# Banded plus pooled attention feeding a ReGLU feed-forward on one core: slot order moved into tables, one more head pair turned by TensorE

## The chip, the cores and the metric

The kernel runs on one core of a Trainium2 chip. The metric is device time in microseconds from the start to the end of one execution. A time is the median of several executions; the profile is that of one execution of its own. The engines go by these names: PE is TensorE (PEld its weight load), DVE is VectorE, ACT is ScalarE, POOL is GpSimd, SP is SyncE, which here only issues DMAs. "Lnnn" is a line of the kernel. Each engine takes its instructions strictly in the order in which the program lists them, so an instruction that waits holds up everything behind it on its engine.

## The reference

```python
def _attn_ref(q, k, v):                    # (8, 8, 576, 64) each: batch, heads, positions, depth
    factor = 4
    q_d = q.reshape(B, H, Sd, factor, D).mean(axis=3)     # likewise k_d, v_d; Sd = 144
    out_d = sm_attn(q_d, k_d, v_d)                        # softmax attention on the means
    out_up = np.repeat(out_d, factor, axis=2)
    mask = np.abs(pos[:, None] - pos[None, :]) < factor
    scores = np.where(mask, scale * q @ k^T, -1e9)
    out_local = softmax(scores) @ v
    return out_up + out_local

def _moe_ref(x, w_gate, w_val, w_out):     # x: (4608, 512), the heads side by side
    gate = np.maximum(x @ w_gate, 0.0)     # w_gate, w_val: (512, 1536)
    val = x @ w_val
    return gate * val @ w_out              # w_out: (1536, 512)
```

There are two attentions for every head: a local one over a band seven keys wide, and one over means of four positions whose result is repeated four times. Their sum, 4608 tokens by 512, goes through a gated feed-forward net.

## The kernel before

**Pairs.** The 64 heads are worked on as 32 pairs; pair p holds two heads of batch p // 4, and four pairs make a batch. The attention output goes transposed into one SBUF tensor, xT (512 depths by 4608 tokens), from which the feed-forward net reads.

**Two kinds of pairs.** Q and K come from memory with positions on the partitions and have to be transposed, and so do the softmax weights. For pairs p < NPE = 12 TensorE does both (turn_qk_pe, L281: twelve transposes of 96 columns and their copies out of PSUM; turn_en_pe, L521: six transposes of the local weights; turn_ad_pe, L530: five of the pooled weights). For the other pairs a DMA transposes (turn_qk, L272, and turn_a, L513, both issued by SP). TensorE pairs also add the band mask on PE (one matmul a head, L343), which for the others is an addition on DVE (mask_l, L398), and they get the means of V from PE matmuls (pool_v, L373) where the others load V a second time in another layout (load_v4, L223) and add on POOL (sum_v4, L231). For the first NPP = 5 pairs the means of q and k are also made by PE (twelve more small matmuls in turn_qk_pe); from pair 5 on POOL makes them (pool_qk, L325: two additions, L331 and L334).

**Stages of a pair.** load, load_v (SP); cast_qk for q (on ACT, L257, or on POOL, L259, for pairs 2 to 4) and for k (POOL, L259); cast_v (POOL, L270); the turn of q and k; pool_qk; scores (36 small matmuls, L348); scores_d (four, L365); pool_v (L381, L390); shift_l (DVE: maximum and subtraction); copy_vd (ACT); max_d (DVE); exp_l (ACT); exp_d in two halves (ACT); sums and weights_l (DVE); weights_d (a reciprocal on DVE and two multiplications on POOL, L491); the turns of the weights, each with its copy on ACT (L528, L535); outputs (36 small matmuls, L544, then eight or twelve of the pooled part, L567, and a copy on ACT, L575); add_x (DVE, into xT).

**Slots.** One Python function, slot(n), lists the instructions for n from -2 to 33, and the tile framework is told to keep that order on every engine. Slot n works on the scores and softmax of pair n, on casts and turns of pairs n + 1 to n + 3, on loads of pairs up to n + 5, and on the outputs of pair n - 1 (TensorE pairs) or n - 2 (DMA pairs). SP's queue in a slot holds the DMA transposes first, then the loads of one pair (four pieces of q and k for a TensorE pair, then the V windows), then V and the second V of a DMA pair, then the stores of finished rows.

**The feed-forward net.** The 4608 tokens are nine chunks of 512 columns. An h block (ffn_h, L595) is eight matmuls of 512 columns into two PSUM banks for one of the twelve blocks of 128 hidden units of one chunk, a relu on ACT (L608) and a product on DVE (L610). A y block (ffn_y, L614) is twelve matmuls of 512 columns for 128 finished tokens, a copy on ACT (L632) and a store. A list, ffn, gives their order: three h blocks of a chunk, then one y block of the chunk before. ffn_do (L654) takes the next one, or does nothing if the chunk's tokens are not all there: chunk c needs the batch in which its last token lies (`made`, counted in pairs). A slot calls it up to `quota` times (L688: 0 before slot 4, 3 up to slot 13, then 4 or 5), at fixed places; a None in the list uses up a call. What is left after slot 33 runs by itself.

**Weights.** POOL issues the DMAs of the feed-forward weights, which also change the type: a quarter of w_gate and w_val in each of slots 1 to 4 (load_h_weights, L152), a quarter of w_out in each of slots 5 to 8 (load_y_weights, L160), both at the end of POOL's work for the slot.

**Warm-up.** In slots -1 to 3, fill (L681) puts matmuls on a tile of ones between the stages: twelve in slot -1, five in each of slots 0 to 3. They compute nothing that is used.

Of the kernel before, what the change touches and what calls it, by code (L numbers as in the profile page):

```python
# [17 lines left out]
NEG = -1.0e30  # L18
VR = 112


def _np_constants():
# [18 lines left out]
    both = np.concatenate([mask.reshape(96, 228), np.eye(96, dtype=np.float32)], axis=1)  # L41
    both = (both.view(np.uint32) >> 16).astype(np.uint16).view(np.float32)
    return both, pool, np.eye(96, dtype=np.float16)
# [7 lines left out]
def kernel(  # L51
# [23 lines left out]
    NPE = 12  # L75
    NPP = 5

    mask_np, pool_np, eye_np = _np_constants()
    eye_dr = nc.inline_tensor(eye_np, name="eye96").ap()
    mask_dr = nc.inline_tensor(mask_np, name="band_mask").ap()  # L80
    pool_dr = nc.inline_tensor(pool_np, name="pool4").ap()
# [30 lines left out]
    both_sb = cons.tile([96, 162], FP32, name="both_sb")  # L112
    mask_sb = both_sb.bitcast(BF16)[:, 0:228].rearrange("p (b c) -> p b c", b=6)
    eyeb_sb = both_sb.bitcast(BF16)[:, 228:324]
    pool_sb = cons.tile([VR, 256], FP16, name="pool_sb")
    eye_sb = cons.tile([96, 96], FP16, name="eye_sb")
    warm = cons.tile([128, 2], FP32, name="warm")
    nc.vector.memset(warm, 0.0)
    nc.scalar.dma_start(eye_sb, eye_dr)
    nc.scalar.activation(out=warm, in_=warm, func=AF.Exp)  # L120
    nc.scalar.dma_start(both_sb, mask_dr)
    nc.scalar.dma_start(pool_sb, pool_dr)
# [13 lines left out]
    for t in v_t:  # L136
        nc.gpsimd.memset(t[32:64], 0.0)
    ones = xT[:, 3, 0:TCH]
    nc.vector.memset(ones, 1.0)
    nc.vector.memset(v_t[0][0:32, 0, :], 0.0)  # L140
    for t in qk_t:
        nc.gpsimd.memset(t[:, 2 * S :], 0.0)
    for t in wt_t:
        nc.vector.memset(t, 0.0)
    for t in v4_t:
        nc.vector.memset(t[32:64], 0.0)
# [95 lines left out]
    def cast_qk(p, i):  # L242
# [13 lines left out]
        if i == 0 and not 2 <= p < NPP:  # L256
            nc.scalar.copy(out=dst, in_=src)  # L257
        else:
            nc.gpsimd.tensor_copy(out=dst, in_=src)  # L259
# [21 lines left out]
    def turn_qk_pe(p):  # L281
# [7 lines left out]
        for b in range(3):  # L289
# [5 lines left out]
            if b == 1:  # L295
# [5 lines left out]
                nc.vector.tensor_copy(out=o, in_=tp.rearrange("p f (a g) -> p a g f", a=2))  # L301
# [34 lines left out]
    def scores(p):  # L336
# [3 lines left out]

        if p < NPE:
            for t in sp:
                nc.tensor.matmul(out=t, lhsT=eyeb_sb, rhs=mask_sb, start=True, stop=False)  # L343
# [29 lines left out]
    def pool_v(p):  # L373
        if p >= NPE:
# [56 lines left out]
    def copy_vd(p):  # L431
        s = st[p]
        s["vd"] = p_vd.tile([128, 4, D], FP16, name="vd", tag="vd")
        if p < NPE:
# [349 lines left out]
```

## Time and profile before

| | before |
|---|---|
| median of 3 executions | 394.9 us (394.38 to 395.0) |
| the profiled execution's own time | 394.73 us |
| its span, first to last instruction | 393.0 us |
| mean granted TensorE clock | 0.983 |
| PE busy | 372.9 us, 95%, 4612 matmuls |
| DVE busy | 249.7 us, 64%, 618 instructions |
| ACT busy | 206.1 us, 52%, 580 |
| POOL busy | 198.1 us, 50%, 248 |
| DMA | 65.77 MB in 172204 packets, mean 167 GB/s |

The page cuts the span into 40 equal slices; a digit is the busy share of a slice in tenths, for PEclk the clock that was granted to TensorE, for DMA the mean of the core's 16 engines. The chain is followed back from the last instruction: at each step to what released it, or to the instruction before it on its engine; "issue" is time in which the engine waited for nothing that the profile shows. A row of the timeline is start, length, engine, line, operation, output<-inputs, tile shape, count; a bracket behind it is the idle time before the first of them and what ended it. In the list of waits the three numbers are the total in us, the count and the longest. Matmuls are pipelined, so the start of one to the start of the next tells more than the length of one.

### The profile page before, as it was taken

Reading aid. Unit: us, or ns where it says so; the run is one execution under the profiler, and the core shown is the slowest. Engines: PE = TensorE matmul, PEld = TensorE weight load, DVE = VectorE, ACT = ScalarE, POOL = GpSimd, SP = SyncE. Lnnn points to the kernel's source line nnn. Section 1 sums busy time; section 2 is a strip of 40 time slices with the busy share of each in tenths; the row PEclk is TensorE's granted clock in tenths of the full one; section 3 lists DMA queues with packets and bytes.
Section 4 is the critical chain, followed back from the end, with each engine's and each line's share of the span. In section 5 each row is a group of like instructions: output and inputs, shape, how many; then the busy total and the mean of one; then the engine's idle time right before and its main releaser. Section 6 shows DMA issues by size and latency. Waiting matters only on the chain.

```text
span 393.0 us, 11686 instructions
## 1 busy us (share of the span) xinstructions
PE 372.9 (95%) x4612; PEld 190.7 (49%) x4612; DVE 249.7 (64%) x618; ACT 206.1 (52%) x580; POOL 198.1 (50%) x248
## 2 busy tenths in 40 slices
PE   6997889899999999999999999999999999999996
PEld 3675356555554444444444444444444444444443
DVE  4799469888678868775767777777776322232210
ACT  3687468878664555655555555555445323332321
POOL 5598297865689775757475667757631000000000
PEclk9799699999999999999999999999999999999999
DMA  7999999998999999999999999997322000100102
GB/s 187 244 214 218 224 203 248 220 220 185 201 216 227 228 220 243 228 213 217 221 225 218 215 232 229 209 224 143 98 71 73 28 28 30 50 28 27 48 34 107
DMA packets 172204, 65.77 MB, mean 167 GB/s; under 512 B 152742, under 2 KB 165750, under 8 KB 172150
## 3 DMA queue, kind: packets, MB, share of 16 engines
q1 hardware_dynamic: 165974, 60.18, 72.3%
q0 software_dynamic: 5824, 4.72, 7.9%
q8 instruction: 36, 0.59, 0.7%
q10 hardware_dynamic: 352, 0.14, 0.2%
q14 instruction: 18, 0.15, 0.1%
HBM read 48.50 MB, written 9.44 MB: 147 GB/s over the span
## 4 chain that ended last, share of the span: by engine, by line
PE 71%; DMA 13%; DVE 4%; ACT 4%; POOL 3%; issue 2%; SPq 2%; POOLq 0%; ACTq 0%; DVEq 0%
PE h_ps L600 41%; PE y_ps L622 23%; DMA vst<-in_v_dram 9%; DMA nat<-in_k_dram 3%; PE s_ps L348 2%; SPq L182 2%; PE u_ps L544 2%; PE o_ps L567 1%; PE d_ps L365 1%; DVE sm L424 1%; ACT r L608 1%; POOL h L259 1%; DVE mx L423 1%; DVE g L610 1%; DVE s_ps L401 1%
## 5 line engine op out<-in xcount | busy, mean ns | idle before, releaser
L610 DVE TENSOR_TENSOR g<-r,h_ps 128x512 f16<-128x512 f16 x108 | 73.9, 684 | 102.2 <-PE h_ps L600 69.2
L600 PE MATMUL h_ps<-xT,wg_sb 128*128 128x512 f16 x432 | 112.9, 384 | 0.5 <-DVE sm L424 0.5
L600 PE MATMUL h_ps<-xT,wv_sb 128*128 128x512 f16 x432 | 111.8, 382 | 0.6
L622 PE MATMUL y_ps<-wo_sb,g 128*128 128x512 f16 (+1 forms) x444 | 98.5, 374 | 0.2 <-DVE sm L424 0.2
L608 ACT ACTIVATE r<-h_ps 128x512 f16<-128x512 f32 x108 | 64.2, 595 | 39.0 <-PE h_ps L600 38.8
L600 PEld LDWEIGHTS <-wv_sb 128*128 128x128 f16 x432 | 42.3, 98 | 54.4 <-issue 5.3
L622 PEld LDWEIGHTS <-g 128*128 128x128 f16 x444 | 43.0, 98 | 49.6 <-DVE sm L424 0.3
L600 PEld LDWEIGHTS <-wg_sb 128*128 128x128 f16 x432 | 38.5, 98 | 44.0 <-issue 1.7
L499 POOL TENSOR_TENSOR wts<-ed,rd 80x288 f16<-80x288 f16 x40 | 25.8, 663 | 65.4 <-ACT h L257 31.4
L632 ACT COPY y_sb<-y_ps 128x512 f32<-128x512 f32 (+1 forms) x36 | 20.8, 578 | 57.9 <-PE y_ps L622 57.7
L460 ACT ACTIVATE e<-sm 96x456 f16<-96x456 f32 x32 | 18.6, 583 | 58.2 <-DVE sm L424 55.0
L448 ACT ACTIVATE ed<-d_ps,nb 80x144 f16<-80x144 f32 x128 | 47.4, 381 | 0.0
L270 POOL CAST v<-vst 112x1152 f16<-112x1152 f32 x32 | 36.8, 1151 | 12.2 <-DMA vst<-in_v_dram 12.2
L331 POOL TENSOR_TENSOR t<-qkT 128x576 f32<-128x576 f16 x27 | 30.9, 1144 | 6.3 <-DVE qkT L301 5.3
L259 POOL CAST h<-nat 96x768 f16<-96x768 f32 x35 | 29.3, 836 | 5.6 <-DMA nat<-in_k_dram 2.8
L407 DVE TENSOR_REDUCE d_ps<-d_ps 80x2 f32<-80x288 f32 x64 | 28.9, 452 | 1.5 <-PE d_ps L365 1.5
L584 DVE TENSOR_TENSOR xT<-u_ps,od 128x288 f16<-128x288 f32 x64 | 26.0, 445 | 2.9 <-ACT od L575 2.9
L257 ACT CAST h<-nat 96x768 f16<-96x768 f32 x29 | 24.3, 841 | 5.4 <-DMA nat<-in_k_dram 5.4
L423 DVE TENSOR_REDUCE mx<-s_ps 96x6 f32<-96x228 f32 x64 | 24.3, 379 | 3.8 <-PE s_ps L348 3.8
L424 DVE TENSOR_TENSOR sm<-s_ps,mx 96x228 f32<-96x228 f32 x64 | 25.1, 391 | 2.2
L448 ACT ACTIVATION_READ_ACCUMULATOR ed<-d_ps,nb 80x1 f32 x128 | 26.2, 205 | 0.0
L472 DVE TENSOR_TENSOR wts<-e,rl 96x456 f16<-96x456 f16 x32 | 25.1, 786 | 1.1
(59 smaller groups left out, 369.4 us busy)
## 6 DMA issues: line engine op xcount, KB each, us to landing
vst<-in_v_dram SPq DMA_DIRECT2D x62, 216.0 KB, 4.8
out_dram<-y_sb SPq DMA_DIRECT2D x35, 256.0 KB, 3.8
nat<-in_q_dram SPq DMA_DIRECT2D x20, 288.0 KB, 3.7
nat<-in_k_dram SPq DMA_DIRECT2D x20, 288.0 KB, 4.5
v<-in_v_dram SPq DMA_DIRECT2D x40, 144.0 KB, 4.2
nat<-in_q_dram SPq DMA_DIRECT2D x12, 192.0 KB, 5.9
nat<-in_k_dram SPq DMA_DIRECT2D x12, 192.0 KB, 4.8
wg_sb<-in_moe_w_gate_dram POOLq DMA_DIRECT2D x4, 384.0 KB, 8.8
```

The source lines that it names most:

```text
L259: nc.gpsimd.tensor_copy(out=dst, in_=src)
L270: nc.gpsimd.tensor_copy(out=s["v16"], in_=s.pop("vst"))
L331: nc.gpsimd.tensor_tensor(out=t1, in0=qkv[:, :, :, 0], in1=qkv[:, :, :, 1], op=ALU.add)
L407: nc.vector.tensor_reduce(out=nbr, in_=s["dp"][h], axis=AX.X, op=ALU.max)
L423: nc.vector.tensor_reduce(out=mx[:, half], in_=sp, axis=AX.X, op=ALU.max)
L424: nc.vector.tensor_tensor(out=sm[:, half, :], in0=sp, in1=mx[:, half, None].to_broadcast([96, 6, 38]), op=ALU.subtract,)
L448: nc.scalar.activation(out=s["ed"][:, i, :], in_=s["dp"][h][:, c, :], func=AF.Exp, scale=SCALE / 16.0, bias=s["nb"][:, i : i + 1], accum_o ...
L584: nc.vector.tensor_tensor(out=x5[:, :, par], in0=up[par].rearrange("p l (t f) -> p l t f", f=4), in1=od4[:, :, par, :, None].to_broadcast( ...
L600: nc.tensor.matmul(out=h, lhsT=w[:, kk, bass.ts(jj, 128)], rhs=xT[:, kk, bass.ts(c, TCH)], start=(kk == 0), stop=(kk == 3),)
L608: nc.scalar.activation(out=r, in_=h1, func=AF.Relu)
L610: nc.vector.tensor_tensor(out=g, in0=r, in1=h2, op=ALU.mult)
L622: nc.tensor.matmul(out=y, lhsT=gts[c][jj][:, bass.ts(ty, 128)], rhs=wo_sb[:, jj, cols], start=(jj == 0), stop=(jj == NJJ - 1),)
```

## The change

**The order is data.** slot(n) no longer calls the stages one by one. Three tables of words, FIRST for n < 4, MIDDLE for 4 <= n < NPE and LAST for the rest, list the stages; a word names a stage, an offset to n and, behind a colon, whether it applies only to TensorE pairs or to DMA pairs. In MIDDLE several stages stand elsewhere than before: scores_d behind turn_en and pool_v; turn_ad ahead of turn_qk_pe; pool_qk of DMA pairs and their transposes first; load_v of a DMA pair behind the slot's scores, and in LAST ahead of the next q/k load; exp_l behind the first feed-forward call; weights_l behind add_x on DVE.

**Split stages.** weights_d becomes the reciprocal (rd) and the products (scale_d); outputs becomes the 36 small matmuls (outputs) and the pooled part (outputs_d).

**Thirteen pairs.** NPE is 13, so pair 12 is turned by TensorE with its mask on PE; it still gets the means of V from a second load and POOL (NPV = 12).

**Casts and copies.** The q cast runs on POOL for pairs 2, 3, 6, 7, 8 and 10 (before: 2, 3 and 4), on ACT for all others. One of the three copies of turned q/k moves from DVE to ACT for pairs 3 and 6.

**Chunks.** Seven chunks of 512 columns, then 448, 288 and 288: chunk 7 ends with batch 6, and batch 7 is two chunks. A narrower block has the same matmuls with fewer columns. A y block is now listed by its 128 tokens alone, wherever these lie among the chunks; there is no None in the list any more. When the next h block's tokens are not there, ffn_do may take a later y block of tokens that are already through.

**Quotas and weights.** The number of calls of ffn_do has its own entry for every slot from 4 to 33. The four quarters of w_gate and w_val are asked for in slots 0, 2, 3 and 4 (in the order 0, 2, 1, 3), those of w_out in slots 5 to 8 (0, 3, 1, 2).

**Constants and warm-up.** The band mask, a bfloat16 identity and the pooling matrix arrive in one DMA instead of two, and the memsets are listed in another order. The warm-up matmuls are 12 in slot -1, then 3, 7, 5 and 3.

```diff
+FIRST = """
+        loads store fill=a scores scores_d turn_en-1:pe pool_v mask shift copy_vd exp_l max_d
+        cast_pool+2:pe cast_v+2:pe fill=b turn_qk_pe+1:pe turn_ad-1:pe exp_d0 fill=c
+        outputs-1:pe outputs_d-1:pe fill=d sums weights_l x-1:pe exp_d1 cast_act+2:pe
+        pool_qk+1:pe rd scale_d weights
+"""
+MIDDLE = """
+        pool_qk+1:dma turn_qk+2:dma loads scores load_v+4:dma v4load+4 store turn_en-1:pe
+        pool_v scores_d mask cast_pool+2:pe shift copy_vd max_d ffn exp_l turn_ad-1:pe
+        turn_qk_pe+1:pe outputs-1:pe outputs_d-1:pe exp_d0 sums v4sum+2 x-1:pe weights_l
+        cast_act+3:dma ffn exp_d1 rd cast_v+2:pe pool_qk+1:pe cast_act+2:pe scale_d
+        cast_pool+3:dma weights cast_v+2:dma ffn ffn ffn
+"""
+LAST = """
+        turn_a-1:dma turn_qk+2:dma load_v+4:dma loads v4load+4 store scores scores_d
+        turn_en-1:pe pool_v mask shift copy_vd exp_l max_d pool_qk+1:dma ffn turn_ad-1:pe
+        exp_d0 outputs-1:pe outputs_d-1:pe outputs-2:dma outputs_d-2:dma sums weights_l x-1:pe
+        x-2:dma exp_d1 ffn rd scale_d cast_act+3:dma cast_pool+3:dma cast_v+2:dma v4sum+2 ffn
+        ffn ffn
+"""
+FILL = {"a": {-1: 12, 1: 2}, "b": {0: 1, 1: 3, 2: 3, 3: 1}, "c": {0: 1, 1: 1, 2: 1, 3: 1}, "d": {0: 1, 1: 1, 2: 1, 3: 1}}
...
-    NPE = 12
+    NPE = 13
     NPP = 5
+    NPV = 12
...
-        if i == 0 and not 2 <= p < NPP:
+        if i == 0 and p not in (2, 3, 6, 7, 8, 10):
             nc.scalar.copy(out=dst, in_=src)
...
-                nc.vector.tensor_copy(out=o, in_=tp.rearrange("p f (a g) -> p a g f", a=2))
+                if p in (3, 6):
+                    nc.scalar.copy(out=o, in_=src)
+                else:
+                    nc.vector.tensor_copy(out=o, in_=src)
...
+    chunks = [(TCH * c, TCH) for c in range(7)] + [(7 * TCH, 448), (4032, 288), (4320, 288)]
...
-                    rhs=xT[:, kk, bass.ts(c, TCH)],
+                    rhs=xT[:, kk, t0 : t0 + nt],
...
+        while nt:
+            n = min(nt, TCH - t0 % TCH)
+            if (t0 // TCH, jj) not in gts:
+                gts[t0 // TCH, jj] = p_g.tile([128, TCH], FP16, name="g", tag="g")
+            lo = chunks[c][1] - nt
+            nc.vector.tensor_tensor(
+                out=gts[t0 // TCH, jj][:, t0 % TCH : t0 % TCH + n],
+                in0=r[:, lo : lo + n],
+                in1=h2[:, lo : lo + n],
+                op=ALU.mult,
+            )
+            t0, nt = t0 + n, nt - n
...
+    for c, (t0, nt) in enumerate(chunks):
+        for i in range(NJJ):
+            ffn.append(("h", c, i))
+            if i % 3 == 2 and 128 * ys + 128 <= t0:
+                ffn.append(("y", ys))
+                ys += 1
+    ffn += [("y", i) for i in range(ys, NTOK // 128)]
...
+    quota = (3, 2, 2, 2, 3, 2, 2, 3, 5, 2, 5, 5, 4, 4, 4, 5, 4, 5, 5, 4, 4, 4, 5, 4, 3, 5, 3, 3, 3, 5)
...
+        blocks = quota[n - 4] if 4 <= n < 34 else 0
+        for name, off, kind in _order(FIRST if n < 4 else MIDDLE if n < NPE else LAST):
...
+            elif name == "weights":
+                i = {0: 0, 2: 2, 3: 1, 4: 3, 5: 4, 6: 7, 7: 5, 8: 6}.get(n)
+                if i is not None:
+                    (load_h_weights if i < 4 else load_y_weights)(i % 4)
```

More of the change, by code (lines that the diff above doesn't have):

```diff
@@ L111 @@
     cons = pool("consts", 1)
[L112 to L115, printed above, removed]
+    cons_sb = cons.tile([VR, 290], FP32, name="cons_sb")
+    mask_bf = cons_sb[0:96, 0:162].bitcast(BF16)
+    mask_sb = mask_bf[:, 0:228].rearrange("p (b c) -> p b c", b=6)
+    pool_sb = cons_sb[:, 162:290].bitcast(FP16)
     eye_sb = cons.tile([96, 96], FP16, name="eye_sb")
     warm = cons.tile([128, 2], FP32, name="warm")
[L118 to L122, printed above, removed]
     p_v16 = pool("v16", 5)
@@ L373, in pool_v @@
     def pool_v(p):
[L374 removed]
+        if p >= NPV:
             return
@@ new lines, in load_more, with part @@
+    def load_more(n):
+        ahead = 5 if n < NPE - 2 else 6
+        while loaded[0] < min(NP, n + ahead):
+            p = loaded[0]
+            load(p)
+            if p < NPE:
+                load_v(p)
+            loaded[0] += 1
+    def part(f, *a):
+        return lambda p: f(p, *a)
+    stages = dict(
+        turn_a=turn_a, turn_qk=turn_qk, scores=scores, scores_d=scores_d, turn_en=turn_en_pe,
+        turn_ad=turn_ad_pe, pool_v=pool_v, mask=mask_l, shift=shift_l, copy_vd=copy_vd,
+        exp_l=exp_l, max_d=max_d, cast_act=cast_qk_act, cast_pool=cast_qk_pool, cast_v=cast_v,
+        pool_qk=pool_qk, turn_qk_pe=turn_qk_pe, exp_d0=part(exp_d, 0), exp_d1=part(exp_d, 1),
+        outputs=outputs, outputs_d=outputs_d, sums=sums, weights_l=weights_l, x=x_stage, rd=weights_d, scale_d=scale_d,
+        load_v=load_v,
+    )
@@ L746 @@
+    prepare()
     with tc.manual_schedule():
```

208 lines of the change are left out of this document (96 added, 112 removed).

## The prediction, on record before the changed kernel ran

> **What bounds the kernel now.** I read the page's slices first, then the busy time of three stretches, then the chain of waits in order of time, then the list of who waited for whom, then single slots on the timeline.
>
> ```profile
> PE   6997889899999999999999999999999999999996
> PEclk9799699999999999999999999999999999999999
> DMA  7999999998999999999999999997322000100102
> ```
>
> One slice is 9.8 us. PE is at 8 or 9 tenths from the fifth slice on, the granted clock dips twice, both times before 49 us, and the DMA engines are full until slice 28.
>
> ```profile
> 0.00:51.00 51.00, 39.84 (x713) 25.53 (x713) 34.44 (x88) 29.77 (x87) 32.23 (x45) 0.87 1.08 216
> 51.00:105.00 54.00, 50.78 (x920) 32.28 (x917) 43.88 (x109) 41.55 (x119) 40.59 (x49) 1.00 1.08 214
> 105.00:393.00 288.00, 282.28 (x2988) 132.88 (x2987) 171.40 (x422) 134.82 (x376) 125.28 (x156) 1.00 0.71 150
> ```
>
> The columns are busy time of PE, weight load, DVE, ACT and POOL, then clock, DMA share and GB/s. PE idles 11.2 us before 51 us, 3.2 us between 51 and 105, and 5.7 us in the 288 us after that. So there are three stages: a front that something else than PE sets, the slots whose pairs TensorE turns (slots 5 to 12), and 288 us that are PE work and nothing else. The chain of waits says what sets the front and what the end:
>
> ```profile
> 30.04 17.51 DMA vst<-in_v_dram
> ...
> 47.82 0.99 issue
> 48.81 1.14 POOL t L331
> ...
> 50.03 0.67 POOL qkd L334
> ...
> 371.30 5.18 PE h_ps L600 x24
> 376.47 10.37 PE y_ps L622 x48
> ```
>
> The second V load of pair 6 lands at 30.04 + 17.51 = 47.55 us. POOL takes its instructions in order and stands at the cast of that tile; behind it is the pooling of pair 5 (L331, L334), and scores_d of pair 5 on PE needs that. I call 50.7 us, when it starts, the anchor: the front can move by a lot without moving it.
>
> ```profile
> POOL v L270 <- DMA vst<-in_v_dram: 12.2, 6, 7.8
> PE o_ps L567 <- ACT at L535: 3.3, 8, 1.0
> PE d_ps L365 <- POOL qkd L334: 2.8, 1, 2.8
> ```
>
> The longest of POOL's six waits for V, 7.8 us, is the one before the anchor; 2.8 us of it reach PE. PE's other frequent wait is 3.3 us in eight pieces: outputs (L567) waits until ACT has copied the weights that turn_ad (L534) transposed just before. One slot of the middle stage, PE alone:
>
> ```profile
> 57.51 0.36 PE L343 MATMUL s_ps<-both_sb 96*96 96x228 bf16 x2
> 57.80 0.43 PE L348 MATMUL s_ps<-qkT 64*32 64x38 f16 x36
> 58.16 0.32 PE L365 MATMUL d_ps<-qkd 64*80 64x144 f16 x4
> 58.41 0.43 PE L527 MATMUL a_ps<-eye_sb,wts 96*128 96x96 f16 x6
> 58.68 0.61 PE L381 MATMUL v_ps<-v,pool_sb 112*128 112x128 f16 x8
> 59.22 0.25 PE L390 MATMUL v_ps<-v,pool_sb 112*64 112x64 f16 x4
> 59.40 1.04 PE L600 MATMUL h_ps<-xT,wg_sb 128*128 128x512 f16 x4
> 60.28 1.03 PE L600 MATMUL h_ps<-xT,wv_sb 128*128 128x512 f16 x4
> 61.14 0.68 PE L292 MATMUL t_ps<-eye_sb,h 96*128 96x96 f16 x12
> 61.65 0.34 PE L534 MATMUL a_ps<-eye_sb,wts 80*128 80x80 f16 x5
> 61.93 0.57 PE L544 MATMUL u_ps<-at,v 38*64 38x32 f16 x36
> 62.82 0.44 PE L567 MATMUL o_ps<-at,vd 128*64 128x80 f16 x8 [0.32 <-ACT at L535]
> 63.19 1.04 PE L600 MATMUL h_ps<-xT,wg_sb 128*128 128x512 f16 x4
> 64.07 1.03 PE L600 MATMUL h_ps<-xT,wv_sb 128*128 128x512 f16 x4
> 64.93 0.36 PE L343 MATMUL s_ps<-both_sb 96*96 96x228 bf16 x2
> ```
>
> The reader is to see start-to-start costs: mask 0.29, six transposes 0.27, four scores_d 0.25, pool_v 0.72, twelve transposes 0.51, five 0.28, a feed-forward block 1.74 at most. The slot is 7.42 us, and the only hole in it is 0.32.
>
> **The change part by part.** The sum is made against the profiled execution, 394.73 us (span 393.0 and 1.73 around it); the median of the runs shown is 394.9, so 0.17 apart. Runs spread from 394.38 to 395.0, so I take 0.2% (0.8 us) as what can be told from no change.
>
> *scores_d later, at the anchor.* turn_en and pool_v of slot 5 now stand ahead of scores_d.
>
> ```profile
> 47.50 0.43 PE L348 MATMUL s_ps<-qkT 64*32 64x38 f16 x36
> ...
> 50.74 0.32 PE L365 MATMUL d_ps<-qkd 64*80 64x144 f16 x4 [2.81 <-POOL qkd L334]
> 51.00 0.43 PE L527 MATMUL a_ps<-eye_sb,wts 96*128 96x96 f16 x6
> ...
> 51.99 1.04 PE L600 MATMUL h_ps<-xT,wg_sb 128*128 128x512 f16 x4
> ```
>
> They fill the hole before 50.74 (PE is free from 47.93), and the block that started at 51.99 starts at 51.00: -1.0 us. In the other slots scores_d does not wait, and the new place gives POOL that 1.0 us more.
>
> *turn_ad before turn_qk_pe.* Between turn_ad and outputs now stand twelve transposes (0.51) and u_ps (61.93 to 62.50, less than 0.57); ACT copies turn_ad's tile ahead of the q/k tiles, not behind them. So the 3.3 us go, -3.3. Ends: 0, if ACT comes no sooner because the relu now also precedes exp_l; -3.3, all of it. I take the far end, because the longest ordinary hole, 0.32, is smaller than the 0.51 that is put in front.
>
> *Casts of pairs 6, 7, 8 and 10 from ACT to POOL, pair 4's from POOL to ACT.* One costs what POOL's own cast costs. It stands between pool_qk and scale_d, so in slots 4, 5, 6 and 8 the weights of turn_ad, the next V cast and the next pooling come later.
>
> ```profile
> L259 POOL CAST h<-nat 96x768 f16<-96x768 f32 x35 | 29.3, 836 | 5.6 <-DMA nat<-in_k_dram 2.8 <-DMA vst<-in_v_dram 2.7
> 57.51:64.93 7.42, 7.10 (x138) 4.64 (x137) 6.71 (x18) 6.15 (x19) 5.94 (x7) 1.00 1.23 252
> ```
>
> POOL was busy 5.94 of 7.42 us; with 0.84 more it is 6.78 of the 7.1 us to which the slot shrinks. That is hidden, barely. Only at the anchor, where POOL starts late, is something left: scores_d of slot 6 follows four more POOL steps and the two weight issues, and PE, now 1.3 us earlier, meets it. I take +0.5; ends 0 and +0.84 for one cast uncovered.
>
> *Pair 12 turned by TensorE.* PE gets a mask (0.29), six and six transposes (0.27, and 0.28 for five, so 0.34) and twelve (0.51): +1.4. Its two DMA transposes and two DVE mask additions go; neither was on PE's path there. Copies on ACT and pooling stay hidden by slots of 5.5 units of feed-forward.
>
> *Last 1024 tokens as 448, 288 and 288 columns.* 36 h blocks instead of 24 for the same columns, 96 more matmuls, 24 more relus and products. In the chain 24 full matmuls take 5.18 us, 0.216 each; 48 of y take 10.37, of which 24 have half the columns: (10.37 - 36 x 0.216)/24 = 0.108, just half. Narrow ones cost nothing extra there: +0.1, ends 0 and +0.5. All narrow blocks stand behind the last slot, where ACT and DVE have room, so that batches end with chunks does not let a block in earlier.
>
> *Quotas and weights.* In the instruction order of the two programs the blocks done by the end of any slot up to 12 (a y block counted as one and a half) are never more than one and a half apart, and slot 4 still runs only two. The slots with DMA-turned pairs keep their order, but load_v goes ahead of the next q/k load on SP's queue, so a V load may come earlier and a q/k load one V load (4.8 us, below) later; PE idles only 5.7 us in the last 288, so there is little that a late load could already cost, and little to win: 0, ends +-0.5. Two warm-up matmuls fewer: hidden before the anchor.
>
> The first pair of h weights is asked for in slot 0 instead of slot 1, the third still at the end of slot 3.
>
> ```profile
> 25.07 0.93 POOL L155 DMA_DIRECT2D wg_sb<-in_moe_w_gate_dram  x1
> ...
> 38.28 0.75 POOL L155 DMA_DIRECT2D wv_sb<-in_moe_w_val_dram  x1
> vst<-in_v_dram SPq DMA_DIRECT2D x62, 216.0 KB, 4.8
> wv_sb<-in_moe_w_val_dram POOLq DMA_DIRECT2D x4, 384.0 KB, 11.4
> ```
>
> Weights and loads share full DMA engines: a V load takes 4.8 us in the median, and 17.51 beside weights. No FFN block waits for weights, so asking sooner gains nothing by itself. What counts is when V of pair 6 lands. The third set's second half starts at 38.28, by the median it lands at 49.7; V lands before that. Upper bound: V comes only with it, 49.7 - 47.55 = +2.1. Lower bound: V comes so early that PE is the limit; then scores_d starts after s_ps, turn_en and pool_v at 47.93 + 0.99 = 48.9, which is -1.8 more. I take 0, since the same bytes are asked for before V's landing in both.
>
> [...]
>
> Sum: -1.0 - 3.3 + 0.5 + 1.4 + 0.1 = -2.3, so 394.73 - 2.3 = 392.4 us.
>
> **The rivals.**
> 1. *The front moves too.* V of pair 6 lands early because the first weights are out of its way: -1.8 more, 390.6. For it: slot 1 asks for no weights any more. Against: the bytes are the same.
> 2. *Weights hold V up.* +2.1: 394.5, no change that can be told. For it the 17.51 us; against, that the third set keeps its place.
> 3. *POOL becomes the bound in slots 4 to 8, slower.* If POOL's slot gets longer than PE's, each moved cast shows: scores_d waits for pool_qk. It decides once POOL needs over 7.1 us a slot; now it has 5.94 + 0.84. Price 4 x 0.84 = 3.4 in place of the 0.5: 392.4 + 2.9 = 395.3; with half of the 3.3 lost to the same lateness 396.9. For it: 0.3 us of slack a slot.
> 4. *The waits stay.* ACT reaches turn_ad's copy as late as before, because relu and exp_l now come in one piece ahead of it: 392.4 + 3.3 = 395.7. For it: ACT is busy 6.15 of 7.42 us. Against: four casts leave it.
>
> **How the numbers follow.** Chances: forecast 0.50 (own range 390.9 to 393.8), rival 1 0.17, rival 2 0.10, rival 3 0.11, rival 4 0.12. Predicted 392.4. Range 389.2 to 396.4: below, rival 1 with 1.4 us for holes among the 5.7 us after 105; above, between rivals 3's two prices. Faster by over 0.2% (under 394.1): 0.48 + 0.17 + 0.02 = 0.67. Within it: 0.02, 0.08 and 0.04 of rivals 3 and 4, 0.14. Slower: the rest of them, 0.19.
>
> **What would show it.** The anchor: scores_d of pair 5 again near 50.7, with turn_en and pool_v before it. The list of waits: o_ps on ACT under 1 us in total; no new d_ps on POOL beyond slots 5 and 6 (else rival 3). Middle slots with two blocks last 7.1 us. The landing of pair 6's V at 47.5: 49 or later is rival 2. PE idle after 105 us still about 5.7. The forecast is wrong if the 288 us stage shortens: nothing that I found does that.

## The result, and the profile after

The changed kernel takes 390.49 us in the median of six executions (389.55 to 392.33) beside 394.87 us for the kernel before, a ratio of 0.9899 with a 95% interval of 0.9868 to 0.9931: 2.7 to 5.2 us faster. In a second set on another occasion it was 391.3 against 395.5 us, 0.9906 [0.987, 0.9942]. The prediction was 392.4 us in a range of 389.2 to 396.4, so the direction and the range held, the median lies just under the likeliest case's own range (390.9 to 393.8), and the gain of 2.3 us was too small by about 2.

The profiled execution took 390.11 us with a span of 388.3. Its slices:

```profile
PE   7598898999999999999999999999899999999996
PEclk9969899999999999999999999999999999999999
DMA  8999999999899999999999999998505001011002
```

PE is at 9 tenths from slice 8 on, one slice earlier than before, but for slice 29 and the last; DMA stays full up to slice 28, and the clock still dips twice in the front. To see where the time came from, both programs are cut where equal work is done. The start of slot 5 and the start of slot 9 are such points (2 and 11 h blocks are done at either in both programs); a slot's start is its first score or mask matmul on the timeline. Windows of the kernel before, then of the changed one (time, then busy time of PE, weight load, DVE, ACT and POOL, clock, DMA share, GB/s):

```profile
0.00:47.22 47.22, 38.87 (x671) 24.93 (x672) 32.37 (x83) 29.77 (x87) 29.01 (x41) 0.86 1.09 217
47.22:82.17 34.95, 30.20 (x557) 19.22 (x556) 28.25 (x69) 25.16 (x73) 27.76 (x33) 1.00 1.13 226
82.17:117.31 35.14, 33.37 (x545) 19.58 (x543) 27.25 (x69) 25.49 (x73) 23.89 (x29) 1.00 0.99 206
117.31:292.17 174.86, 173.22 (x2213) 81.38 (x2213) 131.93 (x343) 95.38 (x289) 116.15 (x145) 1.00 1.02 203
292.17:393.00 100.83, 97.24 (x633) 45.58 (x632) 29.91 (x54) 30.34 (x60) 1.29 (x2) 1.00 0.14 48
```

```profile
0.00:46.96 46.96, 37.62 (x668) 23.54 (x669) 31.62 (x82) 29.41 (x88) 30.44 (x44) 0.89 1.10 217
46.96:78.60 31.64, 30.06 (x557) 18.85 (x556) 28.55 (x68) 23.33 (x71) 28.34 (x35) 1.00 1.22 227
78.60:114.89 36.29, 35.70 (x565) 20.86 (x563) 27.92 (x69) 26.45 (x75) 28.26 (x35) 1.00 1.12 209
114.89:289.25 174.36, 172.18 (x2225) 82.09 (x2224) 133.53 (x343) 96.88 (x291) 111.30 (x138) 1.00 1.03 203
289.25:388.30 99.05, 95.58 (x721) 54.27 (x720) 31.95 (x77) 31.41 (x71) 2.16 (x4) 1.00 0.16 50
```

The five rows are the front, slots 5 to 8, slots 9 to 12, slots 13 to 30, and the rest. The front is 0.26 us shorter, slots 5 to 8 are 3.31 shorter. Slots 9 to 12 are 1.15 longer but do one h block more, 1.74 us, so they gained 0.59; slots 13 to 30 do the same blocks in 0.50 less; the rest does that one h block less and is otherwise equal. From the start of slot 9 to the end it is 310.83 against 309.70, 1.13 less. The sum is 4.7, the difference of the spans.

Slots 5 to 8 can be followed on the timeline to the last tenth. PE's own work in them is 29.94 us. Before, 2.87 came on top at the anchor (the start-to-start of the wait that the list gives as 2.8) and 2.14 in four waits of o_ps: 34.95. After, both are gone and 1.70 us of something new stands there: 31.64. PE in slot 5, the changed kernel:

```profile
47.25 0.43 PE L397 MATMUL s_ps<-qkT 64*32 64x38 f16 x36
47.62 0.43 PE L581 MATMUL a_ps<-eye_sb,wts 96*128 96x96 f16 x6
...
48.60 0.32 PE L414 MATMUL d_ps<-qkd 64*80 64x144 f16 x4
48.85 1.04 PE L663 MATMUL h_ps<-xT,wg_sb 128*128 128x512 f16 x4
```

No bracket: scores_d waits for nothing, and the first block of the slot starts at 48.85, not 51.99. From PE's lines in the list of waits of the changed kernel:

```profile
PE h_ps L663 <- DVE xT L643: 1.7, 2, 1.1
PE a_ps L581 <- DVE wts L521: 1.6, 2, 1.3
PE o_ps L626 <- ACT at L590: 1.4, 4, 0.5
```

The wait of d_ps for POOL has left the list, that of o_ps for ACT fell from 3.3 to 1.4, and two waits for DVE are new. The second of them is in slots 6 and 7. Its larger part, at the start of slot 7, then what DVE and POOL did just before (their work of slot 6):

```profile
63.43 0.43 PE L581 MATMUL a_ps<-eye_sb,wts 96*128 96x96 f16 x6 [1.30 <-DVE wts L521]
```

```profile
60.15 0.82 DVE L643 TENSOR_TENSOR xT<-u_ps,od 128x288 f16<-128x288 f32 x2
60.89 2.49 DVE L521 TENSOR_TENSOR wts<-e,rl 96x456 f16<-96x456 f16 x1
```

```profile
60.63 1.14 POOL L313 CAST v<-vst 112x1152 f16<-112x1152 f32 x1 [1.55 <-DMA vst<-in_v_dram]
61.74 1.14 POOL L378 TENSOR_TENSOR t<-qkT 128x576 f32<-128x576 f16 x1
62.96 0.94 POOL L381 TENSOR_TENSOR qkd<-t 128x288 f16<-128x288 f32 x1
```

weights_l, which takes 0.63 us in most slots, takes 2.49: it is issued at 60.89, during POOL's cast of V, and ends at 63.38, half a microsecond after POOL's first pooling step ended at 62.88. turn_en of slot 7, at 63.43, needs it. In this profile the 2.49 us run beside two POOL operations in a row, the cast (1.14 us) and the first pooling step (1.14 us); what holds weights_l that long is not shown.

### The profile page after: what moved, and what is told of

Read it like the earlier page. It is cut to its first block, busy times and chain, and to the rows that moved or that the text cites. A ratio compares the mean times of both kernels' runs of the same rounds, so it can differ in the third digit from the quotient of the medians.

```text
span 388.3 us, 11986 instructions
## 1 busy us (share of the span) xinstructions
PE 371.1 (96%) x4732; PEld 199.6 (51%) x4732; DVE 253.6 (65%) x639; ACT 207.5 (53%) x595; POOL 200.5 (52%) x251
## 4 chain that ended last, share of the span: by engine, by line
PE 85%; DVE 7%; DMA 3%; ACT 2%; POOL 2%; issue 1%; SPq 1%; POOLq 0%; ACTq 0%; DVEq 0%
PE h_ps L663 47%; PE y_ps L694 23%; PE u_ps L599 3%; PE s_ps L397 3%; PE o_ps L626 2%; PE d_ps L414 2%; DMA vst<-in_v_dram 1%; DVE wts L521 1%; PE t_ps L335 1%; DMA nat<-in_k_dram 1%; DVE xT L643 1%; PE a_ps L581 1%; PE v_ps L430 1%; DVE sm L473 1%; DVE g L677 1%
## 5 line engine op out<-in xcount | busy, mean ns | idle before, releaser
L677 DVE TENSOR_TENSOR g<-r,h_ps 128x512 f16<-128x512 f16 (+4 forms) x132 | 76.7, 589 | 97.0 <-PE h_ps L663 59.7
L663 PE MATMUL h_ps<-xT,wg_sb 128*128 128x512 f16 (+2 forms) x480 | 114.6, 361 | 1.7 <-DVE xT L643 1.7
L663 PE MATMUL h_ps<-xT,wv_sb 128*128 128x512 f16 (+2 forms) x480 | 113.4, 359 | 0.0
L671 ACT ACTIVATE r<-h_ps 128x512 f16<-128x512 f32 (+2 forms) x120 | 66.6, 555 | 52.2 <-PE h_ps L663 50.2
L663 PEld LDWEIGHTS <-wv_sb 128*128 128x128 f16 x480 | 47.1, 98 | 49.3 <-issue 3.7
L694 PEld LDWEIGHTS <-g 128*128 128x128 f16 x444 | 42.0, 98 | 45.9
L663 PEld LDWEIGHTS <-wg_sb 128*128 128x128 f16 x480 | 43.9, 98 | 41.6 <-issue 0.5
L302 POOL CAST h<-nat 96x768 f16<-96x768 f32 x38 | 31.3, 824 | 4.7 <-DMA nat<-in_k_dram 4.7
L521 DVE TENSOR_TENSOR wts<-e,rl 96x456 f16<-96x456 f16 x32 | 26.9, 841 | 0.8
L300 ACT CAST h<-nat 96x768 f16<-96x768 f32 x26 | 21.8, 837 | 5.0 <-DMA nat<-in_k_dram 5.0
```

Of the source, the lines that this page charges most:

```text
L521: nc.vector.tensor_tensor(out=s["en"][:, :, 0:38], in0=s.pop("e"), in1=s.pop("rl")[:, :, None].to_broadcast([96, 12, 38]), op=ALU.mult,)
L663: nc.tensor.matmul(out=h, lhsT=w[:, kk, bass.ts(jj, 128)], rhs=xT[:, kk, t0 : t0 + nt], start=(kk == 0), stop=(kk == 3),)
L671: nc.scalar.activation(out=r, in_=h1, func=AF.Relu)
L677: nc.vector.tensor_tensor(out=gts[t0 // TCH, jj][:, t0 % TCH : t0 % TCH + n], in0=r[:, lo : lo + n], in1=h2[:, lo : lo + n], op=ALU.mult,)
L694: nc.tensor.matmul(out=y, lhsT=gts[ty // 4, jj][:, bass.ts(ty % 4, 128)], rhs=wo_sb[:, jj, cols], start=(jj == 0), stop=(jj == NJJ - 1),)
```

## The experiments

Medians of one set are against the kernel before on the same chip. It soon showed that executions of one kernel spread over several microseconds. In the profiles nearly all of that lies before slot 9, which starts between 78.11 and 82.73 us, while the time from slot 9 to the end repeats within 0.1 us (309.69 to 309.77 in the four profiles that do the same work there as the changed kernel, 310.83 and 310.84 in two of the kernel before). So the stretches of each profile say more than the medians, and both are given.

**The changed kernel again.**

> The changed kernel once more, as the measure for the runs beside it. Expected 390.5 us, 4.4 us under the kernel before; scores_d of pair 5 starts at 48.6 us as in its first profile, after V of pair 6 landed at about 44.

Measured 391.3 us, but the profiled execution took 394.23. Windows up to slot 5, slots 5 to 8, and the rest:

```profile
0.00:44.66 44.66, 35.15 (x668) 23.02 (x669) 30.47 (x82) 29.15 (x88) 28.00 (x40) 0.92 1.06 210
44.66:82.73 38.07, 31.30 (x557) 19.20 (x556) 26.16 (x68) 23.35 (x71) 31.27 (x37) 0.91 1.13 222
82.73:392.50 309.77, 303.46 (x3509) 157.19 (x3507) 193.38 (x489) 154.75 (x436) 141.74 (x175) 1.00 0.75 153
```

POOL and PE in slot 5 of this execution:

```profile
50.09 1.14 POOL L313 CAST v<-vst 112x1152 f16<-112x1152 f32 x1 [8.11 <-DMA vst<-in_v_dram]
```

```profile
53.14 0.46 PE L414 MATMUL d_ps<-qkd 64*80 64x144 f16 x4 [6.77 <-POOL qkd L381]
```

The same program has the anchor back: V of pair 6 was cast at 50.09, not 43.99, and scores_d waited 6.77 us, after the fastest front of all (44.66). So the anchor is a race between PE and a load that lands at different times, and the first profile had simply won it. In the fourteen profiles of this text scores_d of slot 5 waits for POOL in two only: the first of the kernel before and this one. From slot 9 on the two executions differ by 0.07 us.

**The weights, in both kernels.** The old slots in the changed kernel, as below, and the new ones in the kernel before:

```diff
-                i = {0: 0, 2: 2, 3: 1, 4: 3, 5: 4, 6: 7, 7: 5, 8: 6}.get(n)
+                i = {1: 0, 2: 1, 3: 2, 4: 3, 5: 4, 6: 5, 7: 6, 8: 7}.get(n)
```

> The changed kernel with the feed-forward weights asked for in slots 1 to 8 in their old order. Weights theory: the second half of pair 6's V then shares its flight with two and a half sets of weights again, lands near 47 us instead of 43.9, POOL's cast of it holds scores_d of pair 5 at about 50.5 and the time grows by 1.5 to 2.5 us, to about 392.5. Table theory (the front moved because of the order of the stages, not because of the weights): V lands at 44 to 45, the time stays within 0.5 us of the changed kernel.

> The kernel before with only the new slots and order of the weights. Weights theory: V of pair 6 lands near 44 us, scores_d of pair 5 starts 1.5 to 2.5 us earlier than 50.74, the time falls by as much, to 392.4 to 393.4 (the changed place of scores_d is missing here, so not the whole 3.1 us of the front). Table theory: V lands near 47.5 as before and the time stays at 394.9.

The changed kernel with the old slots took 390.68 us (0.9894 [0.9863, 0.9925]; the unaltered one beside it 0.9906), the kernel before with the new slots 395.65 (1.0000 [0.9977, 1.0024]). The weights theory falls: in the first of them V of pair 6 was cast at 44.03, as early as with the new slots, and slots 5 to 8 took 30.75 us; the times did not move either way. The profile of the second:

```profile
47.58:82.26 34.68, 31.86 (x558) 19.67 (x557) 30.03 (x69) 25.24 (x73) 25.40 (x31) 0.95 1.21 229
82.26:393.10 310.84, 303.87 (x3387) 146.60 (x3385) 189.06 (x466) 151.21 (x420) 140.90 (x175) 1.00 0.74 153
```

V of pair 6 was cast at 44.60 here, which by itself fits the weights theory, but 50.09 above, with the same weight slots, does not. Slot 5 had no wait at the anchor, and yet slots 5 to 8 were hardly shorter: scores_d waited some 1.0 us for POOL in slots 6 and 7 instead, the clock was at half for 3.4 us in slot 8, which shows as 1.66 us more of PE's busy time (31.86 against 30.20), and the o_ps waits were all there. Without the clock the stretch would be some 1.9 us shorter than in the first profile (an estimate: 34.95 - 34.68 + 1.66), so this profile doesn't say that an early V is worth nothing in the kernel before; the median says only that the new weight slots are.

**The two moves alone, in the kernel before.** For slots 4 to 11 only:

```diff
-        at_stage(n, scores, scores_d)
+        mid = 4 <= n < NPE
+        at_stage(n, scores, *(() if mid else (scores_d,)))
         at_stage(n - 1, turn_en_pe, pe=True)
...
-        at_stage(n, pool_v, mask_l, shift_l, copy_vd, exp_l, max_d)
+        at_stage(n, pool_v, *((scores_d,) if mid else ()), mask_l, shift_l, copy_vd, exp_l, max_d)
...
-        if 4 <= n < NPE:
+        at_stage(n - 1, turn_ad_pe, pe=True)
+        if mid:
             at_stage(n + 1, turn_qk_pe, pe=True)
-        at_stage(n - 1, turn_ad_pe, pe=True)
```

> The kernel before with two moves of the change alone, in slots 4 to 11: scores_d behind turn_en and pool_v, and turn_ad ahead of turn_qk_pe. By the prediction's own terms both together give -1.0 and -3.3, so 390.6 us or 4.3 under the kernel before, and from the start of slot 9 to the end, 310.83 us in the profile of before, about 1.7 less (the o_ps waits of slots 9 to 12). Rival, that loads and POOL set the time up to slot 9 whatever PE does: from slot 9 on the same 1.7 less, but the start of slot 9 stays at 82 us and the whole gain is under 2 us.

```profile
0.00:50.55 50.55, 39.36 (x670) 24.70 (x671) 34.83 (x83) 29.32 (x87) 33.16 (x46) 0.83 1.10 225
50.55:81.37 30.82, 30.09 (x558) 18.94 (x557) 28.00 (x68) 24.71 (x73) 23.66 (x28) 1.00 1.16 221
81.37:391.80 310.43, 303.69 (x3387) 146.49 (x3385) 189.96 (x468) 151.43 (x421) 141.57 (x175) 1.00 0.74 153
```

In the profile slots 5 to 8 are 4.1 us shorter than in the kernel before and the rest 0.4, where 1.7 was expected. Together that is 4.5 us from slot 5 on, near the two terms, but it can't be put down to the moves alone: V of pair 6 was cast at 42.47, eight microseconds before slot 5 began, so the 2.87 us of the anchor would have been absent with the old order too. In this execution the front was 3.3 us longer, at a clock of 0.83 instead of 0.86. The median, 394.38 against 395.73 us (0.9957 [0.9919, 0.9995], single runs 390.65 to 397.86), has only 1.35 us of it, as the rival said, and slot 9 starts at 81.37. Whether the front of this kernel is longer in every execution, so that the moves need other parts of the change to show, is not settled by one profile.

**turn_ad behind turn_qk_pe again, in the changed kernel.**

```diff
-pool_v scores_d mask cast_pool+2:pe shift copy_vd max_d ffn exp_l turn_ad-1:pe
-turn_qk_pe+1:pe outputs-1:pe
+pool_v scores_d mask cast_pool+2:pe shift copy_vd max_d ffn exp_l turn_qk_pe+1:pe
+turn_ad-1:pe outputs-1:pe
```

> The changed kernel with turn_ad behind turn_qk_pe again in slots 4 to 12. By the prediction's term the waits of o_ps on ACT come back, 0.37 us and more in each of nine slots, together 3.3 us: 393.8 us. Rival, that the time up to slot 9 is set elsewhere: PE has the waits in its list, but only those from slot 9 on (some 2 us) show in the end, 392.5.

Measured 393.74 us, 0.9954 [0.9917, 0.9992]; expected was 393.8. That the median falls so close is partly luck: single runs went from 391.37 to 396.56, and the interval overlaps that of the changed kernel. The list of waits and the last stretch say more:

```profile
PE o_ps L626 <- ACT at L590: 5.6, 11, 1.2
```

```profile
81.71:392.90 311.19, 303.54 (x3509) 157.49 (x3507) 193.01 (x489) 154.59 (x436) 140.84 (x175) 1.00 0.74 153
```

The o_ps waits go from 1.4 to 5.6 us, one in each slot from 4 to 13 and one more in slot 3. From slot 9 on, 1.49 us of them show in full (311.19 against 309.70). This is the best-supported part of the gain.

**Twelve pairs instead of thirteen** (NPE = 12, nothing else; slot 12 then goes by the table LAST instead of MIDDLE).

> The changed kernel with twelve pairs turned by TensorE instead of thirteen. By the prediction's own term pair 12 costs PE 1.4 us and hides nothing, so the time falls to about 389.1. Rival: the DMA-turned pair 12 is late or makes DMA transposes meet the last loads of the TensorE pairs, then the time is the same as that of the changed kernel or up to 1 us longer.

Not faster: 393.64 us, 0.9948 [0.9913, 0.9983], with single runs from 390.81 to 397.13. The stretch from slot 9 and PE in slot 12:

```profile
79.52:389.60 310.08, 302.30 (x3483) 155.71 (x3481) 192.29 (x490) 152.56 (x432) 141.82 (x175) 1.00 0.77 156
```

```profile
106.33 0.34 PE L589 MATMUL a_ps<-eye_sb,wts 80*128 80x80 f16 x5
106.61 0.46 PE L599 MATMUL u_ps<-at,v 38*64 38x32 f16 x36
108.24 0.44 PE L626 MATMUL o_ps<-at,vd 128*64 128x80 f16 x8 [1.16 <-ACT at L590]
```

PE is busy for 302.30 us of it, 1.16 less than with thirteen pairs (303.46, the sum of the last three windows shown first: 35.70, 172.18 and 95.58). That is the predicted price of pair 12, nearly. But the stretch is 0.38 longer, because 1.54 us of idle time are back, most of it in waits of o_ps for ACT's copy: 0.95 us in slot 11 and 1.16 in slot 12, against 0.40 and 0.19 with thirteen pairs. In slot 11 pair 12's q and k transposes no longer stand between turn_ad and outputs, which is the hole that they had filled. Slot 12 has no such transposes with either number. There ACT's exp_l, which LAST puts ahead of the first feed-forward call, waits 1.04 us for DVE, which now has pair 12's mask to add, and the copy of turn_ad stands behind it. So the run prices pair 12 and the table of its slot together. The rival said the same sign for another reason: the waits of o_ps are for ACT, not for a load.

**weights_l ahead of add_x again.**

```diff
-exp_d0 sums v4sum+2 x-1:pe weights_l
+exp_d0 sums v4sum+2 weights_l x-1:pe
```

> The changed kernel with weights_l ahead of add_x on DVE in slots 4 to 12, as before the change. Theory, that the 1.6 us that PE waited for weights_l in the first profile come from the later start of it, beside POOL's cast of V and pooling, which stretch it from 0.63 to 2.49 us: no wait of turn_en for weights_l longer than 0.3 us in the profile, slots 6 and 7 take 7.05 us each if V is there in time. Rival, that POOL alone is late: waits of d_ps on POOL or of turn_ad on scale_d appear in their place. From slot 9 to the end the same 309.7 us within 0.3.

Measured 392.63 us, 0.993 [0.9892, 0.9969]. PE's waits:

```profile
PE a_ps L581 <- DVE xT L643: 1.1, 2, 0.6
PE d_ps L414 <- POOL qkd L381: 0.9, 2, 0.7
PE a_ps L581 <- DVE wts L521: 0.3, 1, 0.3
```

The wait for weights_l fell from 1.6 to 0.3, as the theory wanted, and came back as 1.1 for add_x and 0.9 for POOL: slots 5 to 8 took 31.50 against 31.64, and the stretch from slot 9 grew to 310.42. In slot 6 weights_l now came first (59.87, 0.63 us); POOL's cast of V of pair 8 began at 60.10 and took 1.41 us instead of 1.14, and scores_d of slot 7 waited 0.66 for POOL. In slot 7 weights_l (67.65) met the cast of V of pair 9 (66.89) and the pooling behind it, took 2.00 us, and held up add_x. So weights_l met POOL's work with either of DVE's two stages first, and one of the two took longer: the cast by 0.27 us in slot 6, weights_l by 1.37 in slot 7. The rival is the nearer.

**The old set of q casts on POOL** (pairs 2, 3 and 4).

> The changed kernel with the old set of q casts on POOL (pairs 2, 3 and 4; pairs 6, 7, 8 and 10 back on ACT). By the prediction's term the casts on POOL cost 0.5 us at slot 6: slots 5 to 8, 31.6 us in the first profile of the changed kernel, take 0.5 less, and if POOL was the limit there (the prediction's third rival) up to 1.7 less, down to 29.9, where PE has no wait; the time is 390.0 or 388.8. Rival, that ACT has no room: waits of o_ps on ACT's copies come back in slots 5 to 10, 0.3 us each or more, and the time is 391 or longer.

Measured 391.02 us, 0.9912 [0.988, 0.9943], no difference to the changed kernel. Slots 5 to 8 in this profile, and in that of the last experiment below, which has the same casts:

```profile
48.90:79.05 30.15, 29.98 (x557) 18.83 (x556) 26.93 (x68) 25.03 (x74) 24.67 (x30) 1.00 1.18 229
```

```profile
47.42:79.42 32.00, 30.05 (x557) 18.85 (x556) 28.73 (x68) 25.23 (x74) 26.28 (x32) 1.00 1.23 226
```

They take 30.15 and 32.00 us, so the casts don't decide it: both end at 79 us, and the one that began earlier took longer. ACT took them without new waits: o_ps on ACT 1.1 us.

What decides slot 7 can be read from all ten profiles that have weights_l behind add_x in MIDDLE. The first row is by how much POOL's cast of V of pair 8 starts ahead of slot 7, the second how long turn_en of slot 7 then waits for weights_l:

| | | | | | | | | | | |
|---|---|---|---|---|---|---|---|---|---|---|
| lead of the cast, us | 0.78 | 0.79 | 0.92 | 1.32 | 1.49 | 1.66 | 1.87 | 1.91 | 2.61 | 2.63 |
| wait of turn_en, us | 1.30 | 1.29 | 1.17 | 0.76 | 0.59 | 0.44 | 0.23 | 0.17 | 0 | 0 |

Where there is a wait, the two add up to 2.08 to 2.10 us: turn_en starts 2.80 to 2.82 us after the cast, which is the cast and one pooling step (2.25) and half a microsecond, whatever else the run changed. The old casts have a lead of 1.91 in one profile and 0.92 in the other. So the cause of the new wait is a late V of pair 8, not the q casts. It is again in part a race with a load: POOL had stood waiting for that V's DMA in the profiles with 0.78, 0.92 and 1.32.

**No weights asked for in slot 3**, then also with uniform chunks.

```diff
-                i = {0: 0, 2: 2, 3: 1, 4: 3, 5: 4, 6: 7, 7: 5, 8: 6}.get(n)
+                i = {0: 0, 2: 1, 4: 2, 5: 3, 6: 4, 7: 5, 8: 6, 9: 7}.get(n)
```

> The changed kernel with no weights asked for in slot 3: quarters in order in slots 0, 2, 4, 5, then those of w_out in slots 6 to 9. Theory, that what counts for V of pair 6 is how many weight bytes are asked for ahead of its landing, not in which slot: two sets instead of three are in front of it, 0.77 MB less at some 220 GB/s, so it lands 3 us earlier, near 41 us, and V of pairs 7 and 8 too; slots 5 to 8 take 30 to 30.8 us, no execution waits for V of pair 6 as the second profile of the changed kernel did (6.8 us), the median is 389 to 390. Rival, that the chain from slot 4 on is PE's own by now: V lands earlier and POOL only waits less, the time stays at 390.5 to 391.3. Third, that the second quarter, used in slot 5, or the last, used in slot 8, is late: a wait of h_ps for a weight DMA.

> The same with nine chunks of 512 columns: 0.2 us less from the start of slot 9 to the end than the run beside it (309.5 against 309.7), as in the run of uniform chunks alone; up to slot 9 the same.

Measured 391.05 (0.9904 [0.987, 0.9939]), which is the rival's time, and 390.63 us (0.9889 [0.9854, 0.9924]). V of pair 6 was cast at 46.99 and 46.92, not at 41; slots 5 to 8 took 30.49 and 30.22 as expected, but after fronts of 49.33 and 50.59. Fewer weights ahead of it didn't bring that load forward. From slot 9 on they took 310.18 and 310.09 us, some 0.4 more than the changed kernel, because the later weights make scores_d of slot 11 wait 0.37 us for POOL; the uniform chunks gave 0.1 here, not 0.2.

What goes with the length of a front is the clock. The first window, up to the start of slot 5, in the two extremes (the changed kernel again, shown above with 44.66 us at 0.92, and this last kernel):

```profile
0.00:50.59 50.59, 40.93 (x668) 25.90 (x669) 33.74 (x82) 29.98 (x88) 30.10 (x42) 0.80 1.03 204
```

The starts of slot 5 and the mean granted clock up to there, for all fourteen profiles in order of the clock:

| clock | start of slot 5, us |
|---|---|
| 0.92 | 44.66 |
| 0.89 | 46.68, 46.96, 47.42, 47.58 |
| 0.86 | 47.22, 47.36, 47.98, 49.27, 49.40 |
| 0.83 | 48.90, 49.33, 50.55 |
| 0.80 | 50.59 |

Of the three with instructions of the kernel before, 47.22, 47.58 and 50.55, none lies apart from the others. A front at a lower clock tends to end later, whatever kernel it is. No edit here changed the clock by itself, so which causes which is only argued: PE at the half clock ends its work later (four matmuls of 512 columns took 1.73 us start to start from 42.18 in the first profile of the changed kernel, at a clock of 0.50, and 0.86 from 45.24, at 1.00), and a late load leaves PE idle (6.77 us at scores_d in the second). In one place the order can be seen: in the second profile of the changed kernel PE stood idle from 46.4 to 53.1 us, and the granted clock was at half from 49.0 to 56.0, so this dip followed the wait and made it 1.4 us dearer.

**Uniform chunks.** Nine chunks of 512 columns in the changed kernel.

> The changed kernel with nine chunks of 512 columns. By the prediction chunk sizes are worth nothing but 0.1 us for narrower matmuls, so the stretch from the start of slot 9 to the end stays at 309.7 within 0.3. Rival, that ends of chunks with batches count: the two waits of h_ps for the last pair of a batch, 0.70 and 1.20 us in slots 25 and 29, go, but the first block of the last chunk can't start before the last pair, and calls of ffn_do find nothing to do; then the stretch is longer than 309.7 by more than 0.5.

Measured 390.44 us, 0.9883 [0.9846, 0.992]. From slot 9 to the end 309.48 us, 0.22 less than with the narrow chunks. The two waits for the last pair of a batch (0.71 and 1.20 us, start to start) were still there: the quotas put the first block of a chunk right behind add_x, not the sizes.

**The version put together from this.** Uniform chunks, old casts, and two calls of ffn_do moved behind the batch's end:

```diff
-    quota = (3, 2, 2, 2, 3, 2, 2, 3, 5, 2, 5, 5, 4, 4, 4, 5, 4, 5, 5, 4, 4, 4, 5, 4, 3, 5, 3, 3, 3, 5)
+    quota = (3, 2, 2, 2, 3, 2, 2, 3, 5, 2, 5, 5, 4, 4, 4, 5, 4, 5, 5, 4, 3, 5, 5, 4, 2, 5, 4, 3, 3, 5)
```

> The changed kernel with nine chunks of 512 columns, the old set of q casts on POOL (pairs 2, 3 and 4), and two h blocks called one slot later (one fewer call in slots 24 and 28, one more in 25 and 30), so that the first block of chunks 5 and 6 stands behind a block and a y block when it needs the last pair of its batch. From the runs so far: slots 5 to 8 take 30.2 us (31.6 in the first profile of the changed kernel), from slot 9 to the end 309.5 less most of the two waits of 0.71 and 1.20 us, so 307.7 to 308.2. If the front falls as it does on average, the median is 389.0, 1.5 to 2 us under the changed kernel and 6 under the kernel before. Rival: h blocks right behind outputs bring back holes of 0.2 us each on PSUM banks and the later blocks only wait elsewhere; then the last stretch stays at 309.3 or more.

Measured 389.39 us (388.38 to 391.59) against 395.54, 0.9862 [0.9828, 0.9896]. Slots 13 to 30 and the rest:

```profile
115.71:288.88 173.17, 172.24 (x2226) 82.09 (x2225) 134.41 (x343) 96.51 (x290) 112.45 (x139) 1.00 1.03 202
288.88:387.80 98.92, 95.34 (x625) 44.84 (x624) 29.31 (x53) 30.14 (x60) 1.29 (x2) 0.99 0.15 49
```

Slots 5 to 8 took 32.00 us, not the 30.2 that was expected: V of pair 8 was late again. From slot 9 to the end it was 308.38 us (expected 307.7 to 308.2), 1.32 less than in the changed kernel: PE's idle time in slots 13 to 30 fell from 2.18 to 0.93 us, and no wait of h_ps for add_x is left. That part is clear of the scatter. The whole time is 6.2 us under the kernel before; its interval overlaps that of the changed kernel, so that it beats that kernel as a whole is not shown.

## Why the prediction was right, and where it fell short

Its sum was -2.3 us, the profiles differ by 4.6 and the medians by 4.4 and 4.2. The direction was right, and so was one mechanism, that of turn_ad. That the sum came as near as it did is partly luck, because errors in other terms cancelled in part. Term by term:

- *scores_d at the anchor, -1.0.* Too small, and by a wrong idea of the anchor. It was taken as a fixed time that the change could only pack better. In the profile after it was gone, -2.87, because V of pair 6 came in time; in the second profile it cost 6.8. Fourteen profiles show that load cast between 42.5 and 50.1 us. The first rival had the size right (scores_d at 48.9, found 48.60; 390.6 us, found 390.1 to 390.5) and the cause wrong: moving the weights, in both kernels, moved nothing. The second rival is out by the same runs.
- *turn_ad ahead of turn_qk_pe, -3.3.* The mechanism held: undone, the waits came back. All 2.14 us of slots 5 to 8 went. From slot 9 on the waits were 1.3 us before (in slots 9 to 12) and are 1.1 after (0.40, 0.19 and 0.53 in slots 11 to 13), so the net is -1.9 in the list of waits, where some 0.2 of the 1.4 lie in the front. Slots 9 and 10, with a turn of q and k to cover the copy, lost theirs; slots 12 and 13 have no such turn. The fourth rival, that all of the waits stay, is out.
- *Casts on POOL, +0.5.* Mis-placed: the casts decide nothing. What came in the first profile was +1.7 us in slots 6 and 7, through weights_l on DVE, which now stands behind add_x and so meets POOL's work on a late V; in ten profiles that wait is 0 to 1.3 us in slot 7 and follows V. The prediction priced POOL's time and not what weights_l takes beside POOL's work; weights_l stretched to 0.98 and 1.13 us, and to 1.87 in the front, was in the trace of before. The third rival's wait, d_ps on POOL, did not appear.
- *Pair 12, +1.4.* The term that failed in sign. PE's work was sized nearly right (1.16 us), but without it 1.54 us of idle time come back, so it is worth -0.4, together with the order of slot 12.
- *Narrow chunks, +0.1.* Measured +0.2, and +0.1 in the later pair of profiles.
- *Weights, 0, and quotas, 0.* The weights are 0. The quotas were not: slots 13 to 30 gained 0.50 us, made mainly of three parts. From slot 22 on a slot with three h blocks and a y block took 9.40 us before (eight slots) and takes 9.20 now, where the blocks stand in another order; slot 27, 10.41 before, with waits of 0.36 and 0.34 us for DVE, has none now; against it stand the two waits for add_x, 1.9 us. Here are PE's lines behind outputs, the kernel before and the changed one:

```profile
228.06 0.37 PE L567 MATMUL o_ps<-at,vd 48*64 48x80 f16 x12
228.37 1.04 PE L600 MATMUL h_ps<-xT,wg_sb 128*128 128x512 f16 x4
229.45 1.02 PE L600 MATMUL h_ps<-xT,wv_sb 128*128 128x512 f16 x4
```

```profile
225.63 0.37 PE L626 MATMUL o_ps<-at,vd 48*64 48x80 f16 x12
225.94 2.76 PE L694 MATMUL y_ps<-wo_sb,g 128*128 128x512 f16 x12
228.54 1.03 PE L663 MATMUL h_ps<-xT,wg_sb 128*128 128x512 f16 x4
```

The four matmuls into the first bank take 1.08 us start to start behind outputs (228.37 to 229.45), 0.88 in the slot shown with the prediction (59.40 to 60.28). What holds them up isn't shown, and it isn't an h block behind outputs alone: in slot 20 of the kernel before one stands there too, took 0.88 (189.35 to 190.23), and the slot took 9.20. "The forecast is wrong if the 288 us stage shortens" named this risk, and it did shorten.

By place: up to slot 5 the prediction had nothing and 0.26 us came, less than that stretch scatters; for slots 5 to 8 it had -1.0 - 2.14 + 0.5 = -2.6 and -3.3 came; from slot 9 on it had -1.2 (3.3 less 2.14) + 1.4 + 0.1, about +0.3, and -1.1 came. The last is the part that repeats, so the clearest error is there: 1.8 us by pair 12 and 0.5 by the quotas, less the 1.1 of o_ps waits that stayed. That the difference of the profiles comes to 4.6 owes 2.9 to the anchor, which the first profile of before had lost and that of after had won. What repeats is the 2.14 us of o_ps waits in slots 5 to 8 and the 1.13 from slot 9 on, 3.3 us; the other microsecond of the medians lies before slot 9 and no run assigns it.

What stays open: why V of pair 6 lands up to 6 us apart (where POOL waits for it, its cast starts between 43.99 and 50.09), whether the clock dips cause the late fronts or follow them, and why the two moves alone give only 1.35 us in the median. The moved copies of q and k, the order of the V loads, the constants in one DMA and the warm-up were not varied by any run.

## What to carry to other kernels

Work moved onto the bounding engine is not a cost where that engine waits: size the hole that it fills as well as the work, and remember that the hole's cover (here the next pair's transposes) may end with the pair that is moved. A wait at the end of a DMA seen in one execution can be a sample of a race (the same program cast V of pair 6 at 43.99 and at 50.09 us), so look at a second profile before a term is built on it, and cut the programs at points of equal work: the stretches behind the race repeat to 0.1 us where medians scatter by 2. Where a wait is removed by a new order on one engine, look at what then runs beside it; PE did not wait for weights_l in the profile of the kernel before, and does in that of the changed one, where it ends behind POOL's work on a late V.

## What the runs showed of the hardware

The granted clock falls to half in the front of all fourteen profiles, for stretches of about 3.4, 6.8 or 10.2 us (summed from the clock of half-microsecond windows), between 6.8 us in all before slot 5 (the second profile of the changed kernel) and 20.5 (later weights and uniform chunks). The places differ between executions: the first stretch begins at about 8.5 us in the first profile of the kernel before and at about 20.9 in that of the changed kernel. PE is busy for 0.77 to 0.83 of the time up to slot 5. Two of the fourteen profiles have such a stretch later, 6.8 us in slot 5 (the changed kernel again) and 3.4 us in slot 8 (the kernel before with the new weight slots).
